# Rows of the softmax maximum on SP's queue and one slot sooner, and a pool bank for the value products of each unit

## The chip, the cores and the metric

The kernel runs on one core of one Trainium2 chip. Its time is in device microseconds. A core has TensorE (PE in the profile, with PEld for its weight loads), VectorE (DVE), ScalarE (ACT), GpSimd (POOL) and SyncE (SP). SP computes nothing here; it issues DMA transfers. ScalarE can issue transfers too, between its computations.

## The reference

Four layers one after the other on x of 2048 x 512 in float32, each with a layer norm ahead and a residual sum: a spectral mixing layer, an attention layer, and both once more with the same weights.

```
def _A_ref(x, dft_seq_re, dft_seq_im, dft_hid_re, dft_hid_im):
    a = jnp.einsum("bsd,ed->bse", x, dft_hid_re)
    b = jnp.einsum("bsd,ed->bse", x, dft_hid_im)
    y = jnp.einsum("ts,bse->bte", dft_seq_re, a) - jnp.einsum("ts,bse->bte", dft_seq_im, b)
...
for s in range(N):                                   # N = 4 segments of L = 512 rows, H = 32 heads of 16
    qs, ks, vs = q[:, :, s], k[:, :, s], v[:, :, s]
    logits = jnp.einsum("bhqd,bhkd->bhqk", qs, ks) * scale + mask
    p = _softmax(logits, axis=-1)
    a_dot = jnp.einsum("bhqk,bhkd->bhqd", p, vs)
    a_mem = (phi(qs) @ M) / (phi(qs) @ z + 1e-6)
    o = g * a_mem + (1.0 - g) * a_dot
    M, z = M + phi(ks)^T vs, z + sum(phi(ks))
```

The change touches the attention layers alone: the softmax inside a segment.

## The kernel before, in words

**Units and slots.** An attention layer has 4 segments (`NSEG`), in each 4 groups of 8 heads (`NG`, `HG`), and in each group 2 units of 4 heads (`HU`): 32 units a layer, 64 in all. The program is written as generators, and `place(order, gen, *slots)` puts each step of a generator into a numbered slot; the steps of a slot are issued by rising `order`. A unit n has the slots t to t + 9 with t = t0 + 10 n (`SU` = 10), but its steps reach far around them. TensorE executes exactly in this program order (`in_order`, L80). The instructions of the other engines and of the queues are put in order by the framework's planner, which keeps the dependences, goes by program order and by priority (`tc.high_priority`), and plays the program through with estimated durations. Each queue then works strictly in its order: a transfer at the head of SP's queue that waits holds up all behind it.

**The steps of a unit.**
- `stack` (L787), slot t - 22: four transfers on SP (L803) bring 48 rows of query parts and of key parts to each half ("side", at partitions 0 and 64) of the tiles `stkq` and `stkk`. A query tile has three buffers; three key tiles take turns. Two heads share a side.
- `natural_max` (L810), slots t - 18, - 16, - 14, - 12, - 10: TensorE makes the scores with the queries on the partitions (tile `nat`), VectorE masks each block and reduces it to its row minimum of negated scores (L834, tile `mx`, 4 heads x 4 blocks of 128 rows). In slot t - 8 two VectorE operations (L848, L849) write the maximum as a high part and a remainder into `parts` (`mparts` in the profile). The tile has 5 copies of 16 columns; only two are written, the other three hold zeros.
- `max_rows` (L855), slot t - 4 (t - 5 for the very last unit): TensorE turns the 80 columns of `parts` into rows (tile `mT`), ScalarE copies 32 of them to `mt` (L864), and four transfers on ScalarE's queue (L868), one for each side and part, lay them as row 48 or 49 under the queries of `stkq`. The keys have rows of ones there, so the next product subtracts the maximum.
- `softmax_values` (L874), slots t to t + 12: TensorE makes the scores with the keys on the partitions, with the two extra rows (tile `sT`, five rounds in slots t, t + 2, t + 4, t + 6, t + 8); ScalarE clamps the diagonal blocks (L900) and takes the exponential (L901, tile `pT`); GpSimd zeroes above the diagonal (L904). In slot t + 12 the value products (`pv`, L914) gather the 4 heads in one bank of PSUM, each head in 17 of its 32 partitions (16 values and a column of ones, for the row sum), and ScalarE copies the bank to `ot` (L966).
- `output` (L975), slot t + 14: `ot` is turned back, divided by the row sum and weighted.

**What lies between.** The slots are filled with the projections (`proj`, tiles `pqk`, whose split results go out through SP on L779), the values (`values`, `pvv`), the memory terms and the output product (`po`). Loads and stores of rows are on SP as well.

**The value bank.** PSUM has 8 banks in one pool (`bank`, L114). `alloc_pv` (L1146) takes one at the start of an attention layer and clears it on VectorE (L1148); every unit of the layer accumulates into this one bank, and the 15 partitions of each head that no product writes keep the zeros. The other 7 banks go round among all else.

**The values' tile.** `v_all` (L175) holds six row blocks of 32 x 17 numbers; `ones` (L1282) sets the columns of ones on GpSimd at the start of the first attention.

Of the kernel before, what the change touches and what calls it, by code (L numbers as in the profile page):

```python
# [10 lines left out]
F32 = mybir.dt.float32  # L11
# [23 lines left out]
NSLOT = 3  # L35
KROWS = NSLOT * DH
MROWS = 2
MCOPIES = 5
SIDES = (0, 64)
HP = 2  # L40
VW = DH + 1
# [17 lines left out]
def spectral_infini_kernel(  # L59
# [111 lines left out]
    def finish(ps, xr, x_out, i):  # L171
        V.tensor_tensor(out=xr, in0=ps, in1=xr, op=ALU.add)
        nc.sync.dma_start(x_out[i], xr)

    v_all = consts.tile([P, 6, H * VW], F32, name="v_all")  # L175
    v_tiles = [v_all[:, i].rearrange("p (h e) -> p h e", e=VW) for i in range(6)]
    spare = v_all.rearrange("p a b -> p (a b)")[:, : 6 * 512].rearrange("p (a b) -> p a b", b=512)
    v_count = [0]
    max_parts = [
        consts.tile([P, MCOPIES, HU, LT], F32R, name=f"mparts{i}") for i in range(2)  # L180
    ]

    slots = {}
# [496 lines left out]

    def place_attention(x_in, x_out, t0, w_at, out_at):
        ws, xT, vt, o_nat, state, scr, phi, stacks, maxima, outs = ({} for _ in range(10))
        k_stacks, pv_banks = [], []

        def prep(s, n):
            xt = [load_rows(x_in[s * LT + i]) for i in n]
# [24 lines left out]
        def values(s):  # L711
            vt[s] = {}
            for i in (0, 1, 3, 2):
                ps = bank("pvv")
                for d in range(DT):
                    matmul3(
                        ps,
                        lambda h: xT[s][:, h, d, i * P : (i + 1) * P],
                        lambda h: ws["v", d][:, h, :],
                        d == 0,  # L720
                        d == DT - 1,
                    )
                    if d + 1 < DT:
                        yield
                v = v_tiles[v_count[0] % len(v_tiles)]
                v_count[0] += 1
                A.activation(v[:, :, :DH], ps.rearrange("p (h d) -> p h d", d=DH), AF.Copy)
                vt[s][i] = v
                yield
# [80 lines left out]
        def natural_max(s, g, u):  # L810
            qs, ks = stacks[s, g, u, "q"], stacks[s, g, u, "k"]
            mx = sb.tile([P, HU, LT], F32, name="mx", bufs=2)

            def scores(*cols):
                banks = [bank("nat") for _ in SIDES]
                views, off = [], 0
                for p, i in cols:
                    n = (i + 1) * P
                    for a, at in enumerate(SIDES):
                        T.matmul(  # L820
                            banks[a][:, off : off + n],
                            qs[at : at + KROWS, p, i * P : (i + 1) * P],
                            ks[at : at + KROWS, p, :n],
                            start=True,
                            stop=True,
                        )
                        h = a * HP + p
                        views.append((banks[a][:, off : off + n], mx[:, h, i : i + 1]))
                    off += n
                for src, dst in views[::2] + views[1::2]:  # L830
                    n = src.shape[1]
                    junk = sb.tile([P, 512], BF16, name="junk", bufs=1)
                    with tc.high_priority(offset=URGENT):
                        last_max[0] = V.tensor_tensor_reduce(  # L834
                            junk[:, :n], src, mask[:, 512 - n :], 1.0, 3e38,
                            ALU.add, ALU.min, dst,
                        )

            for p in range(HP):
                scores((p, 3))  # L840
                yield
                scores((p, 0), (p, 2))
                yield
            scores((0, 1), (1, 1))
            yield
            parts = max_parts[((s * NG + g) * (HG // HU) + u) % 2]
            with tc.high_priority(offset=2 * URGENT):
                V.tensor_scalar(parts[:, 0], mx, -1.0, None, op0=ALU.mult)  # L848
                V.scalar_tensor_tensor(  # L849
                    parts[:, 1], mx, -1.0, parts[:, 0].bitcast(F32), op0=ALU.mult, op1=ALU.subtract  # L850
                )
            maxima[s, g, u] = parts
            yield

        def max_rows(s, g, u):  # L855
            qs, parts = stacks[s, g, u, "q"], maxima.pop((s, g, u))
            pt = bank("mT")
            T.transpose(
                pt[: MCOPIES * HU * LT, :P], parts.rearrange("p a h i -> p (a h i)").bitcast(F32), ident
            )  # L860
            n = MROWS * HU * LT
            mt = sb.tile([P, P], F32R, name="mt", bufs=2)
            with tc.high_priority(offset=URGENT):
                A.activation(mt[:n], pt[:n, :P], AF.Copy)  # L864
            for a, at in enumerate(SIDES):
                for r in range(MROWS):
                    j = (r * HU + a * HP) * LT
                    nc.scalar.dma_start(  # L868
                        qs[at + KROWS + r : at + KROWS + r + 1].rearrange("p h s -> p (h s)").bitcast(F32),
                        mt[j : j + HP * LT].bitcast(F32),  # L870
                    )
            yield

        def softmax_values(s, g, u):  # L874
# [39 lines left out]
            def pv(pv_bank, kt, pt, off):  # L914
                n = 512 - kt * P
                for h in range(HU):
                    T.matmul(
                        pv_bank[32 * h : 32 * h + VW, kt * P :],
                        vt[s][kt][:, h0 + h, :],
                        pt[h % HP][:, h // HP, off : off + n],  # L920
                        start=kt == 0,
                        stop=kt == 2,
                        skip_group_check=True,
                    )
# [32 lines left out]
            ev(0, third)  # L957

            def last():
                pb = pv_banks[0]  # L960
                pv(pb, 0, p0, 0)
                pv(pb, 1, p1, 0)
                pv(pb, 3, p1, 384)
                pv(pb, 2, [p2[0][:, :, p] for p in range(HP)], 0)
                ot = sb.tile([P, 512], F32, name="ot", tag="ut", bufs=8)
                A.activation(ot, pb, AF.Copy)  # L966
                outs[s, g, u] = ot
# [175 lines left out]
            finish(ps, xr, x_out, s * LT + i)  # L1143
            yield

        def alloc_pv():  # L1146
            pv_banks.append(bank("pv_bank"))
            V.memset(pv_banks[0], 0.0)  # L1148
            yield

        def alloc_out(s):
            o_nat[s] = [pair("onat", "wd", 8, F32) for _ in range(LT // 2)]
            yield
# [7 lines left out]
        def unit(n):  # L1161
            return n // USEG, n % USEG // NU, n % NU
# [11 lines left out]
        for k in range(4 * DT):  # L1174
            n, d = "qkvo"[k // DT], k % DT
            src = rows((wq, wk, wv, wo)[k // DT], d)
            place(3, load_split(ws, (n, d), src, f"w{n}", "w", 16), [w_at(k) - 3, w_at(k)])
        place(0.1, alloc_pv(), [t0])
        for n in range(NSEG * USEG):
            t = t0 + SU * n  # L1180
            place(0, softmax_values(*unit(n)), run_from(t, 13))
            place(1.9, output(*unit(n)), [t + 14])
            place(1.9, max_rows(*unit(n)), [t - (5 if x_out is out_tiles and n == NSEG * USEG - 1 else 4)])
            place(1, natural_max(*unit(n)), run_from(t - 18, 5, 2), [t - 8])
            place(0.5, stack(*unit(n)), [t - 22])
        for s in range(NSEG):
            b = t0 + SS * s
# [65 lines left out]
    def setup():  # L1253
        nonlocal ident, mask, same_head, gate
        with tc.issue_after(later[0].ins):
            ident = consts.tile([P, P], F32, name="ident")
            make_identity(nc, ident)
            mask = consts.tile([P, 512], BF16, name="mask")
            G.memset(mask, 0.0)
            G.affine_select(  # L1260
                mask[:, 384:], mask[:, 384:], pattern=[[-1, P]], compare_op=ALU.is_ge,
                fill=MASK, base=0, channel_multiplier=1,
            )
            same_head = consts.tile([P, HG], F32, name="same_head")
            V.tensor_reduce(
                same_head, ident.rearrange("p (d h) -> p h d", h=HG), op=ALU.add, axis=mybir.AxisListType.X
            )

            for t in max_parts:
                G.memset(t[:, MROWS:].bitcast(F32), 0.0)  # L1270
            gate = consts.tile([P, 2, H], F32, name="gate")
            beta_b = consts.tile([P, H], F32, name="beta_b")
            nc.sync.dma_start(beta_b, beta[None, :].to_broadcast([P, H]))
            eb = beta_b
            A.activation(eb, beta_b, AF.Exp, scale=-1.0)
            V.tensor_scalar_add(eb, eb, 1.0)
            V.reciprocal(gate[:, 0], eb)
            V.tensor_scalar(gate[:, 1], gate[:, 0], -1.0, 1.0, op0=ALU.mult, op1=ALU.add)
        yield

    ident = mask = same_head = gate = None
    def ones():  # L1282
        for v in v_tiles:
            G.memset(v[:, :, DH:], 1.0)
        yield

    place(5, setup(), [200])
# [46 lines left out]
```

## Time and profile before

| | us |
|---|---|
| time, median of 3 runs | 2052.89 |
| lowest and highest | 2046.74, 2054.2 |
| the profiled execution's own time | 2052.54 |
| its span, first to last instruction | 2050.8 |
| TensorE busy | 1854.5 |
| VectorE busy | 1390.6 |
| ScalarE busy | 1079.4 |
| GpSimd busy | 356.0 |

Both spectral layers and both attentions stand in this span one after another; the attentions fill about 430 to 1020 us and 1450 us to the end. In a line of the profile a name such as `sT<-stkq,stkk` gives the tile that is written and those that are read. "PE sT L84 <- DMA stkq<-mt" in a list of waits reads: TensorE, about to write `sT`, stood idle until a transfer from `mt` to `stkq` had landed; behind it stand the sum in us, the number of times, and the longest. "ACTq" and "SPq" are transfers being issued by ScalarE's and SP's sequencers; such a line lasts as long as the issue, not until the data has landed. "PEclk" and the granted clock are the share of the full clock that TensorE was given.

### The profile page before, as it was taken

The page shows a single profiled execution, that of the slowest core. Times are in us where ns is not written, and L with a number is a line of the kernel's source. Part 1 is how long each engine was busy: PE and PEld are TensorE (multiplying, and loading weights), DVE is VectorE, ACT ScalarE, POOL GpSimd, SP SyncE. Part 2 cuts the span into 40 slices and gives each one's busy share as a digit, 9 for nine tenths or more (in the row PEclk, how much of TensorE's full clock was granted, in tenths as well). Part 3 has the DMA queues.
Part 4 walks back from the last instruction along what each step waited for, and adds up shares of the span by engine and source line. Part 5 has one row for each costly group of instructions (what it writes and reads, how often), then busy time and mean ns, then how long its engine had stood idle before and what let it go on. Part 6 is the DMA issues. An engine that isn't in the chain of part 4 may idle for free.

```text
span 2050.8 us, 32671 instructions
## 1 busy us (share of the span) xinstructions
PE 1854.5 (90%) x10192; PEld 1308.2 (64%) x10192; DVE 1390.6 (68%) x4116; ACT 1079.4 (53%) x2388; POOL 356.0 (17%) x667
## 2 busy tenths in 40 slices
PE   8999999997889889887899999999878898898878
PEld 6888778874455555554578878888545555565444
DVE  8988878745567658656678986575565576676554
ACT  3344434326666556555564664443356575566544
POOL 1000000022222223324210000002122232332222
PEclk9999999998899989998899999999988999899878
DMA  8777753544433434334467776555443353253331
GB/s 278 256 256 237 247 184 122 175 144 135 109 88 114 127 79 130 104 79 115 136 197 239 256 238 194 160 154 166 124 120 98 75 151 99 82 142 101 97 68 37
DMA packets 147292, 303.12 MB, mean 148 GB/s; under 512 B 19888, under 2 KB 23984, under 8 KB 147120
## 3 DMA queue, kind: packets, MB, share of 16 engines
q1 hardware_dynamic: 136112, 287.39, 46.8%
q10 hardware_dynamic: 11008, 13.64, 1.9%
q8 instruction: 82, 1.34, 0.3%
q14 instruction: 90, 0.74, 0.1%
HBM read 211.83 MB, written 88.08 MB: 146 GB/s over the span
## 4 chain that ended last, share of the span: by engine, by line
PE 33%; DMA 5%; ACT 5%; DVE 3%; ACTq 2%; issue 2%; POOL 0%; DVEq 0%
PE m L84 13%; DMA stkq<-mt 5%; PE pv_bank L84 5%; PE y L84 4%; PE pqk L84 3%; ACT pT L901 2%; PE sT L84 2%; PE po L84 2%; ACTq L868 2%; PE pvv L84 1%; PE nat L84 1%; DVE junk L834 1%; ACT sT L900 1%; PE oT L84 0%; PE on L84 0%
## 5 line engine op out<-in xcount | busy, mean ns | idle before, releaser
L834 DVE CUSTOM_DVE_ANT_0 junk<-nat,mask 128x512 bf16<-128x512 f32 (+3 forms) x1024 | 497.2, 486 | 412.4 <-PE nat L84 362.8
L901 ACT ACTIVATE pT<-sT 128x512 f32<-128x512 f32 x640 | 350.0, 606 | 5.7 <-DMA stkq<-mt 5.0
L84 PE MATMUL sT<-stkq,stkk 50*128 50x256 f32 (+3 forms) x1024 | 191.1, 390 | 157.5 <-DMA stkq<-mt 139.3
L904 POOL TENSOR_SCALAR_AFFINE_SELECT pT<-pT 128x256 f32<-128x256 f32 (+1 forms) x448 | 193.2, 445 | 771.4 <-ACT pT L901 622.8
L84 PE MATMUL m<-chi,xa 128*128 128x512 f32 x1056 | 309.1, 393 | 2.7 <-DVE c L524 2.1
L900 ACT ACTIVATE sT<-sT 128x256 f32<-128x256 f32 x625 | 179.6, 329 | 191.4 <-PE sT L84 117.4
L84 PEld LDWEIGHTS sT<-stkq,stkk 50*128 50x128 f32 x1024 | 99.3, 195 | 283.8 <-issue 144.4
L84 PE MATMUL m<-clo,xa 128*128 128x512 f32 x720 | 230.6, 392 | 5.2 <-DVE clo L100 5.2
L84 PEld LDWEIGHTS m<-chi,xa 128*128 128x128 f32 x1056 | 198.0, 188 | 46.8 <-DVE c L524 2.9
L84 PE MATMUL pv_bank<-pT,v_all 128*17 128x512 f32 (+3 forms) x2048 | 188.4, 515 | 0.0
L84 PE MATMUL y<-wdt,us 128*128 128x512 f32 x768 | 182.5, 391 | 0.2 <-DVE wdt L100 0.2
L84 PE MATMUL nat<-stkk,stkq 48*128 48x512 f32 (+3 forms) x1024 | 168.3, 358 | 3.0 <-DVE mx L834 1.8
L84 PEld LDWEIGHTS y<-wdt,us 128*128 128x128 f32 x768 | 143.4, 188 | 30.7 <-DVE wdt L100 0.9
L84 PEld LDWEIGHTS m<-clo,xa 128*128 128x128 f32 x720 | 135.3, 188 | 37.5 <-DVE clo L100 9.8
L98 ACT ACTIVATE chi<-cring 128x512 fp32r<-128x512 f32 (+1 forms) x138 | 99.7, 727 | 85.8 <-PE m L84 35.4
L966 ACT ACTIVATE ot<-pv_bank 128x512 f32<-128x512 f32 x64 | 38.2, 598 | 195.2 <-PE pv_bank L84 195.2
L84 PEld LDWEIGHTS pv_bank<-pT,v_all 128*17 128x17 f32 x2048 | 59.6, 109 | 124.7 <-issue 121.5
L84 PE MATMUL pqk<-xT,wq 128*128 128x512 f32 x384 | 127.7, 457 | 0.0
L84 PE MATMUL pvv<-wv,xT 128*128 128x512 f32 x384 | 126.5, 454 | 0.0
L84 PEld LDWEIGHTS nat<-stkk,stkq 48*128 48x128 f32 x1024 | 110.6, 202 | 20.0 <-issue 5.7
L84 PE MATMUL po<-wo,oh 128*128 128x512 f32 x384 | 119.2, 433 | 1.5 <-ACT mt L864 0.7
L84 PE MATMUL pqk<-xT,wk 128*128 128x512 f32 x384 | 113.5, 425 | 0.8 <-ACT parts L764 0.7
(187 smaller groups left out, 2831.2 us busy)
## 6 DMA issues: line engine op xcount, KB each, us to landing
cring<-in_ct SPq DMA_DIRECT2D x97, 256.0 KB
scrk<-parts SPq DMA_DIRECT2D x96, 256.0 KB
stkq<-scrq SPq DMA_DIRECT2D x128, 192.0 KB
stkk<-scrk SPq DMA_DIRECT2D x128, 192.0 KB
cring<-sum SPq DMA_DIRECT2D x95, 256.0 KB
xt<-mid SPq DMA_DIRECT2D x64, 256.0 KB
scrq<-parts SPq DMA_DIRECT2D x32, 512.0 KB
cring<-in_ct SPq DMA_DIRECT2D x27, 512.0 KB
```

Of the source, the lines that this page charges most:

```text
L84: return tc.keep_in_program_order(op(*args, **kwargs))
L98: pin(A.activation(hi, src, AF.Copy, scale=scale))
L834: last_max[0] = V.tensor_tensor_reduce(junk[:, :n], src, mask[:, 512 - n :], 1.0, 3e38, ALU.add, ALU.min, dst,)
L868: nc.scalar.dma_start(qs[at + KROWS + r : at + KROWS + r + 1].rearrange("p h s -> p (h s)").bitcast(F32), mt[j : j + HP * LT].bitcast(F32),)
L900: A.activation(blocks, blocks, AF.Relu)
L901: A.activation(dst[a], ps, AF.Exp, scale=-SCALE)
L904: G.affine_select(blocks, blocks, pattern=[[0, n] for n in blocks.shape[1:-1]] + [[1, P]], compare_op=ALU.is_ge, fill=0.0, base=0, channel ...
L966: A.activation(ot, pb, AF.Copy)
```

## The change

Three things at once.

1. `max_rows` issues two transfers on SP in place of four on ScalarE's queue. To let one transfer carry both parts of a side, `parts` is laid out by side, part, head and block, so that 16 turned rows in a row belong to one side; the VectorE operations write it with a stride. The tile has 72 columns instead of 80, of which 32 are used as before.
2. `max_rows` stands in slot t - 5 instead of t - 4 (t - 6 instead of t - 5 for the very last unit), and the last step of `natural_max`, the two VectorE operations, in t - 9 instead of t - 8.
3. The value products of each unit take a bank from the pool, and none is held through the layer. So that every partition of it is written, the products use 32 columns of the values, the head's 17 and 15 of the next head's, which nobody reads; `v_all` gets 15 columns of zeros at its end for the last head. The clearing of the bank goes.

```
-MCOPIES = 5
+MCOLS = 72
...
-    v_all = consts.tile([P, 6, H * VW], F32, name="v_all")
+    v_all = consts.tile([P, 6, H * VW + 32 - VW], F32, name="v_all")
...
-        consts.tile([P, MCOPIES, HU, LT], F32R, name=f"mparts{i}") for i in range(2)
+        consts.tile([P, MCOLS], F32R, name=f"mparts{i}") for i in range(2)
...
-                v = v_tiles[v_count[0] % len(v_tiles)]
+                j = v_count[0] % len(v_tiles)
+                v, v_flat[s, i] = v_tiles[j], v_all[:, j]
...
+            sides = mx.rearrange("p (a b) i -> p a (b i)", b=HP)
+            both = parts[:, : MROWS * HU * LT].rearrange("p (a r j) -> p a r j", a=2, r=MROWS)
+            hi, lo = (both[:, :, r] for r in range(MROWS))
...
-                V.tensor_scalar(parts[:, 0], mx, -1.0, None, op0=ALU.mult)
+                V.tensor_scalar(hi, sides, -1.0, None, op0=ALU.mult)
                 V.scalar_tensor_tensor(
-                    parts[:, 1], mx, -1.0, parts[:, 0].bitcast(F32), op0=ALU.mult, op1=ALU.subtract
+                    lo, sides, -1.0, hi.bitcast(F32), op0=ALU.mult, op1=ALU.subtract
                 )
...
-                pt[: MCOPIES * HU * LT, :P], parts.rearrange("p a h i -> p (a h i)").bitcast(F32), ident
+                pt[:MCOLS, :P], parts.bitcast(F32), ident
...
             for a, at in enumerate(SIDES):
-                for r in range(MROWS):
-                    j = (r * HU + a * HP) * LT
-                    nc.scalar.dma_start(
-                        qs[at + KROWS + r : at + KROWS + r + 1].rearrange("p h s -> p (h s)").bitcast(F32),
-                        mt[j : j + HP * LT].bitcast(F32),
-                    )
+                n = MROWS * HP * LT
+                nc.sync.dma_start(
+                    qs[at + KROWS : at + KROWS + MROWS].rearrange("p h s -> p (h s)").bitcast(F32),
+                    mt[a * n : (a + 1) * n].bitcast(F32),
+                )
...
-                        pv_bank[32 * h : 32 * h + VW, kt * P :],
-                        vt[s][kt][:, h0 + h, :],
+                        pv_bank[32 * h : 32 * (h + 1), kt * P :],
+                        v_flat[s, kt][:, (h0 + h) * VW : (h0 + h) * VW + 32],
...
-                pb = pv_banks[0]
+                pb = bank("pv_bank")
...
-        def alloc_pv():
-            pv_banks.append(bank("pv_bank"))
-            V.memset(pv_banks[0], 0.0)
-            yield
...
-        place(0.1, alloc_pv(), [t0])
...
-            place(1.9, max_rows(*unit(n)), [t - (5 if x_out is out_tiles and n == NSEG * USEG - 1 else 4)])
-            place(1, natural_max(*unit(n)), run_from(t - 18, 5, 2), [t - 8])
+            place(1.9, max_rows(*unit(n)), [t - (6 if x_out is out_tiles and n == NSEG * USEG - 1 else 5)])
+            place(1, natural_max(*unit(n)), run_from(t - 18, 5, 2), [t - 9])
...
-        for v in v_tiles:
+        for j, v in enumerate(v_tiles):
             G.memset(v[:, :, DH:], 1.0)
+            G.memset(v_all[:, j, H * VW :], 0.0)
```

More of the change, by code (lines that the diff above doesn't have):

```diff
@@ L173, in finish @@
         nc.sync.dma_start(x_out[i], xr)
-    v_all = consts.tile([P, 6, H * VW], F32, name="v_all")
-    v_tiles = [v_all[:, i].rearrange("p (h e) -> p h e", e=VW) for i in range(6)]
+    v_all = consts.tile([P, 6, H * VW + 32 - VW], F32, name="v_all")
+    v_tiles = [v_all[:, i, : H * VW].rearrange("p (h e) -> p h e", e=VW) for i in range(6)]
     spare = v_all.rearrange("p a b -> p (a b)")[:, : 6 * 512].rearrange("p (a b) -> p a b", b=512)
@@ L682, in place_attention @@
         ws, xT, vt, o_nat, state, scr, phi, stacks, maxima, outs = ({} for _ in range(10))
-        k_stacks, pv_banks = [], []
+        k_stacks, v_flat = [], {}
         def prep(s, n):
@@ L1269, in setup @@
             for t in max_parts:
-                G.memset(t[:, MROWS:].bitcast(F32), 0.0)
+                G.memset(t[:, MROWS * HU * LT :].bitcast(F32), 0.0)
             gate = consts.tile([P, 2, H], F32, name="gate")
```

## The prediction

> **What bounds the kernel now.** I read the page's span first, then the busy time by stage, the waits of TensorE, the tile of the copied maxima, the timeline of one unit and the chain of waits through it.
>
> ```profile
> span 2050.8 us, 32671 instructions
> ```
>
> ```profile
> 430.00:1020.00 590.00, 502.95 (x3194) 311.76 (x3193) 373.68 (x1475) 344.11 (x849) 161.33 (x302) 0.90 0.40 110
> 1020.00:1450.00 430.00, 428.13 (x1945) 346.64 (x1945) 311.72 (x598) 218.34 (x415) 22.78 (x29) 1.00 0.62 198
> 1450.00:2050.80 600.80, 508.75 (x3256) 312.25 (x3255) 361.44 (x1434) 345.99 (x850) 152.29 (x300) 0.89 0.36 99
> ```
>
> The columns are the stage, its length, the busy time of PE, PEld, DVE, ACT and POOL, the granted clock, the DMA share and GB/s. Between the attentions (second row) TensorE is idle for 1.9 us of 430, at clock 1.00. In the two attentions it is idle for 87 and 92 us, at clocks 0.90 and 0.89, and no other engine is busy for more than 64% of them. The change touches attention alone, so the question is what ends these 179 us:
>
> ```profile
> PE sT L84 <- DMA stkq<-mt: 139.3, 70, 4.4
> ...
> PE sT L84 <- ACT phi L756: 4.8, 2, 2.4
> ```
>
> One wait holds 139.3 us: the first softmax scores of a unit wait for the rows of the maximum, 70 times, 2.0 us each. The next in attention has 4.8. Who moves these rows, and how slowly:
>
> ```profile
> L868 ACTq DMA_DIRECT2D stkq<-mt x256: 627/627/1237, 453.1 to 2020.9; - x128
> ```
>
> ```profile
> 1874.97 0.94 PE L84 MATMUL pvv<-wv,xT 128*128 128x512 f32 x3
> ...
> 1877.01 0.31 PE L84 MATMUL mT<-ident,mparts 128*80 128x128 f32 x1
> ...
> 1877.35 0.27 ACT L864 ACTIVATE mt<-mT 32x128 fp32r<-32x128 f32 x1 [0.47 <-PE mT L84]
> ...
> 1878.32 1.97 ACTq L868 DMA_DIRECT2D stkq<-mt  x3
> ...
> 1879.15 0.32 SPq L803 DMA_DIRECT2D stkk<-scrk  x1
> 1879.57 0.88 SPq L803 DMA_DIRECT2D stkq<-scrq  x2
> 1880.50 0.62 SPq L803 DMA_DIRECT2D stkk<-scrk  x1
> ...
> 1884.32 0.47 PE L84 MATMUL sT<-stkq,stkk 50*128 50x256 f32 x3 [1.62 <-DMA stkq<-mt]
> ...
> 1889.16 0.45 PE L84 MATMUL nat<-stkk,stkq 48*128 48x512 f32 x2
> ```
>
> ```profile
> 1879.65 4.53 DMA stkq<-mt
> ...
> 2007.69 2.29 DMA stkq<-mt
> ...
> 2020.93 1.76 DMA stkq<-mt
> ```
>
> The copy ends at 1877.62. The fourth transfer is issued at 1879.65, 2.0 us later, and lands 4.53 after that, at 1884.18. Its landing runs beside the four stack loads that SP issues from 1879.15 to 1881.12. In the last two units, after which no stack is loaded, the same step takes 2.29 and 1.76. So three things make the rows late: four issues in a row, the stack loads beside them, and the late turn.
>
> **The change part by part.**
>
> *One slot sooner.* In TensorE's order the turn moves ahead of slot 5's products and slot 6's scores, by 1877.01 - 1874.97 = 2.04 us. The maxima must be split by then:
>
> ```profile
> 1868.91 0.17 DVE L849 SCALAR_TENSOR_TENSOR mparts<-mx,mparts 128x16 fp32r<-128x16 f32 x1
> ```
>
> They are ready at 1869.08, 5.9 us ahead of the new turn, so the turn waits for nothing new. The two VectorE operations also stand one slot sooner; their count and size stay, so they cost nothing more. On ScalarE the copy (0.27 us) goes ahead of some exponentials; it is the same work in another order.
>
> *Two transfers instead of four, on SP.* ScalarE issues 256 transfers at 0.627 us each, 160 us of its queue in all, and drops them. This gives TensorE nothing by itself, as ScalarE is not the bound. SP takes 128. No row has a transfer of this shape on SP; the nearest are ACT's own 0.627 and this larger one:
>
> ```profile
> L418 ACTq DMA_DIRECT2D sum<-cring x11: 326/327/373, 230.6 to 324.8; - x11
> ```
>
> I take 0.63 (0.33 to 1.25, were it to grow with the doubled rows). In the unit above: turn at 1874.97, copy done by about 1875.8 (ScalarE may finish an exponential first), second issue started by 1876.5, landed 2.3 later, 1878.8, as the stack loads are issued only from 1879.15. TensorE asks for the rows at 1884.32 - 1.62 = 1882.70. Cover: 3.9 us; with a slow landing of 4.53 still 1.7.
>
> The Trainium skill, "DMA: Bandwidth & Descriptors", section "Why a DMA increments its semaphore by 16 and not by 1", speaks against this shape: a transfer is spread over the largest number of engines up to 16 that divides the slowest dimension of both sides. By it one row from eight went over 8 engines, and two rows from sixteen go over 2, eight pieces each in turn. No view here shows the spread of one transfer. If eight pieces in turn doubled the 2.29 us landing, an estimate, the sum would still hold in this unit; only units with less than 2.3 us of cover would pay, at most 64 x 0.5 us or so, and the sum by the page would be some 30 us higher.
>
> *What SP's queue holds.* SP takes its transfers in order, so the rows can stand behind a store that waits, and the stack loads behind the rows.
>
> ```profile
> 1894.17 2.06 SPq L779 DMA_DIRECT2D scrq<-parts  x2
> ...
> 1894.90 0.25 ACT L864 ACTIVATE mt<-mT 32x128 fp32r<-32x128 f32 x1
> ```
>
> ```profile
>   POOL pT L904: 7.0, 2
> ```
>
> In units with a query projection two such stores sit at SP's head until 1894.17 and end at 1896.23. Rows behind them would start there: later than the copy, yet ahead of or level with the fourth issue of today. The stack loads come up to 2 x 0.63 = 1.3 us later; nothing on TensorE waits for them now (who waited for line 803: only the row shown). I set both at nothing. If that cover goes, it is the first rival's price.
>
> *What goes of the wait.* By this cover all 139.3 us can go. I let a quarter come back as other waits (units at either end of an attention, banks, ScalarE's order), a choice: -139.3 x 0.75 = -104.
>
> *The granted clock.* Two units of nearly the same work:
>
> ```profile
> 1850.60:1869.50 18.90, 15.55 (x102) 9.66 (x105) 10.85 (x47) 11.37 (x28) 6.92 (x12) 0.91 0.44 142
> 1886.50:1903.10 16.60, 13.94 (x98) 8.53 (x97) 10.09 (x44) 11.39 (x28) 6.31 (x12) 1.00 0.45 140
> ```
>
> The first is idle for 3.35 us, the second for 2.66. Busy time goes about as one over the clock: 15.55 x 0.91 = 14.2. Were attention at 1.00 as the stage between is, TensorE would save 502.95 x 0.10 + 508.75 x 0.11 = 106 us. With the stalls gone I expect three quarters of it: -80. The Trainium skill, "TensorE: Matmul & The Clock Gate", Part 1, says that the clock halves after an idle window of about 3.4 us. By that, stalls of 2.0 us would hardly lower it, it would not come back with them, and the sum would be 80 us higher. The trace agrees in part: 2.66 idle us left the clock at 1.00 above, yet the stage means are 0.90 and 0.89 with a longest stall of 4.4.
>
> *The value products.* 32 columns of weights instead of 17:
>
> ```profile
> L84 PEld LDWEIGHTS pv_bank<-pT,v_all x2048: 92/98/155, 474.6 to 2039.0; 128*17 128x17 f32 x187
> ```
>
> ```profile
> L84 PEld LDWEIGHTS mT<-ident,mparts x64: 115/118/120, 452.4 to 2017.9; 128*80 128x80 f32 x64
> ```
>
> 80 columns take 118 ns, 17 take 98, so 32 take at most 20 more: 2048 x 0.020 = 41 us if each showed, a quarter of it with four heads side by side, and by the columns' share 15 of 63 about 2.5. The bank is no longer held: the pool has eight for everyone else, but the first value product of a unit may wait for one.
>
> ```profile
> PEld sT L84 <- DVE mx L834: 19.4, 36, 1.9
> ```
>
> Such a weight load waits 0.5 us on the mean now. Bounds: -19 (those waits go) to +64 x 0.5 = +32. I take +5 for both together. The two clears of the bank, the six clears of padding on GpSimd and 72 instead of 80 turned columns: one answer, nothing.
>
> *Sum.* -104 - 80 + 5 = -179. The profiled execution took 2052.54 us (span 2050.8 and 1.7 around it), 0.4 from the median of 2052.89. 2052.5 - 179 = 1873.5, say **1873 us**.
>
> **The rivals.**
>
> *Slower: the rows end up behind the stack loads in SP's order.* Should the planner put them there, they start after 1881.12 and the second at about 1881.8; with 4.53 to land, 1886.3 against 1884.18. That is +2.1 us x 64 = +134, 2187 us, and it decides once the first issue falls behind 1879.15 in most units. For it: that order is the planner's, nobody wrote it. Against it: the copy would be done 3.3 us before these loads are released.
>
> *The next wait takes half.* ScalarE and VectorE are busy for 11.39 and 10.09 us of 16.60 in the fast unit; at 14 us a unit, ScalarE has 81%. And the stack loads have 10.0 us from issue (1879.15) to first use (1889.16), which shrinks by the stall and the clock to 8 or less, with 4.5 or more to land. If half of the wait returns and a third of the clock's share comes: -70 - 35 + 5 = -100, 1952 us.
>
> *The clock stays at 0.90*, because something other than these stalls sets it: -104 + 5, 1953 us. For it: the unit with 2.66 idle us ran at 1.00. Against: the stage between runs at 1.00 with a busier TensorE.
>
> *Nothing moves*: the rows come sooner and another engine's lateness, now hidden behind them, is as long. About 2050. Against it: no wait but this one has over 4.8 us.
>
> **How the numbers follow.** The forecast has 0.64, the two rivals near 1950 together 0.23, no change 0.05, slower 0.08. Of the forecast's own bounds the lower is the whole wait and the whole clock, 2052.5 - 139 - 106 = 1808; the upper, with half of the clock's share and the bank's 32, is about 1930. The range reaches on over the two rivals near 1950, with the value products' remaining bound (41 - 5 = 36): 1808 to 1990. Faster by over 0.5% (about what a measurement of this kernel can tell from no change) is 0.64 + 0.23 = 0.87, within it 0.05, slower 0.08.
>
> **What would show it.** Right: no softmax score waits for the rows, or for under 20 us in all; landing under 3 us from issue; the clock in both attentions above 0.96; both attention stages together near 1191 - 179 = 1012 us. Wrong: issues of the rows behind the stack loads on SP; value products or natural scores that wait for banks or stack loads by over 0.5 us a unit; a clock of 0.90 without the stalls.

## The result, and the profile after

| | before | after |
|---|---|---|
| time, median of 4 runs each, us | 2051.74 | 1786.52 |
| lowest and highest | 2046.74, 2054.2 | 1784.13, 1787.75 |
| the profiled execution | 2052.54 | 1787.75 |
| mean granted clock over the span | 0.940 | 0.993 |

The ratio is 0.8709, 95% interval 0.8689 to 0.8728: 265 us fewer. The forecast of 1873 us had the sign and the mechanism, but 86 us too little of it; 1786.5 lies 21.5 us below the low end of the range, 1808.

First the page's span and busy time, then the stages. The edges are chosen so that each row holds the same number of matmuls, to within four, as its row of before (3194, 1945 and 3256 there).

```profile
span 1786.0 us, 32579 instructions
...
PE 1745.4 (98%) x10192; PEld 1266.5 (71%) x10192; DVE 1383.1 (77%) x4114; ACT 1071.3 (60%) x2388; POOL 357.7 (20%) x673
```

```profile
430.00:890.00 460.00, 450.41 (x3195) 291.48 (x3193) 369.47 (x1473) 339.72 (x847) 163.35 (x303) 0.99 0.53 141
890.00:1320.00 430.00, 428.16 (x1945) 346.73 (x1944) 312.49 (x596) 219.44 (x418) 22.64 (x29) 1.00 0.63 199
1320.00:1786.00 466.00, 452.15 (x3260) 290.78 (x3258) 357.95 (x1437) 342.06 (x850) 152.73 (x300) 0.99 0.48 127
```

The stage between the attentions is the same 430 us. The attentions went from 590.0 + 600.8 to 460 + 466, that is 1190.8 to 926: the whole gain, 264.8, where 1012 was forecast. Inside them TensorE's idle time fell from 87.1 + 92.1 to 9.6 + 13.9, by 155.7, and its busy time from 502.95 + 508.75 to 450.41 + 452.15, by 109.1, at clocks of 0.99 after 0.90 and 0.89. Now the waits of TensorE:

```profile
PE xnT L84 <- DVE xn L168: 6.1, 5, 1.7
PE nat L84 <- DMA stkk<-scrk: 5.6, 8, 2.2
...
PE pv_bank L84 <- DVE mx L835: 1.7, 1, 1.7
...
PE sT L84 <- DMA stkq<-mt: 0.8, 2, 0.5
```

The 139.3 us of waiting for the rows are 0.8, and no wait of that size took their place. The stack loads, for which TensorE never waited before, are now late 8 times, 5.6 us in all. The issues, and a values unit like the one in the prediction:

```profile
L871 SPq DMA_DIRECT2D stkq<-mt x128: 598/617/785, 452.6 to 1758.0; - x128
```

```profile
1652.55 0.27 PE L84 MATMUL mT<-ident,mparts 128*72 128x128 f32 x1
...
1653.31 0.26 ACT L868 ACTIVATE mt<-mT 32x128 fp32r<-32x128 f32 x1
...
1653.60 1.29 SPq L871 DMA_DIRECT2D stkq<-mt  x2
...
1656.66 0.32 SPq L804 DMA_DIRECT2D stkk<-scrk  x1
...
1657.08 0.84 SPq L804 DMA_DIRECT2D stkq<-scrq  x2
...
1657.97 0.41 SPq L804 DMA_DIRECT2D stkk<-scrk  x1
...
1659.84 0.50 PE L84 MATMUL sT<-stkq,stkk 50*128 50x256 f32 x4
```

The copy ends at 1653.57, SP issues both transfers by 1654.89, the first stack load only follows at 1656.66, and the first score runs at 1659.84: 6.3 us after the copy. So it is everywhere: in each of the 64 units SP issues the first of the two within 0.03 us of the end of the copy, and nothing stands ahead of them in its queue. The chain of waits has the landing itself in the last unit alone, beside no stack load:

```profile
1757.36 0.62 SPq L871
...
1758.03 1.92 DMA stkq<-mt
...
1760.09 0.47 PE sT L84 x3
```

### The profile page after: what moved, and what is told of

It is laid out like the page before. It is cut to its first block, busy times and chain, and to the rows that moved or that the text cites. A ratio compares the mean times of both kernels' runs of the same rounds, so it can differ in the third digit from the quotient of the medians.

```text
span 1786.0 us, 32579 instructions
## 1 busy us (share of the span) xinstructions
PE 1745.4 (98%) x10192; PEld 1266.5 (71%) x10192; DVE 1383.1 (77%) x4114; ACT 1071.3 (60%) x2388; POOL 357.7 (20%) x673
## 3 DMA queue, kind: packets, MB, share of 16 engines
q1 hardware_dynamic: 138416, 288.44, 54.7%
q10 hardware_dynamic: 6912, 12.59, 1.8%
## 5 line engine op out<-in xcount | busy, mean ns | idle before, releaser
L84 PE MATMUL nat<-stkk,stkq 48*128 48x512 f32 (+3 forms) x1024 | 159.2, 345 | 8.4 <-DMA stkk<-scrk 5.6
L84 PE MATMUL sT<-stkq,stkk 50*128 50x256 f32 (+3 forms) x1024 | 164.8, 373 | 1.0 <-DMA stkq<-mt 0.8
L84 PEld LDWEIGHTS sT<-stkq,stkk 50*128 50x128 f32 x1024 | 84.4, 186 | 113.4 <-issue 53.0
L84 PE MATMUL pv_bank<-pT,v_all 128*32 128x512 f32 (+3 forms) x2048 | 152.2, 437 | 1.7 <-DVE mx L835 1.7
L84 PEld LDWEIGHTS pv_bank<-pT,v_all 128*32 128x32 f32 x2048 | 59.2, 110 | 84.1 <-issue 82.8
L84 PE MATMUL pqk<-xT,wq 128*128 128x512 f32 x384 | 116.9, 425 | 0.0
L84 PEld LDWEIGHTS nat<-stkk,stkq 48*128 48x128 f32 x1024 | 96.5, 189 | 27.2 <-ACT pT L904 7.7
L147 POOL TENSOR_TENSOR r<-ve,half_neg 128x2 f32<-128x2 f32 (+2 forms) x24 | 19.9, 830 | 472.9 <-DVE ve L145 469.5
L84 PE MATMUL pvv<-wv,xT 128*128 128x512 f32 x384 | 114.1, 417 | 0.0
L84 PE MATMUL pqk<-xT,wk 128*128 128x512 f32 x384 | 108.5, 410 | 2.0 <-DVE mx L835 2.0
```

The costliest lines, as they stand in the source:

```text
L84: return tc.keep_in_program_order(op(*args, **kwargs))
L147: G.tensor_tensor(out=r, in0=ve, in1=half_neg[:, :n], op=ALU.pow)
```

## The experiments

The theory: lateness of the rows at the head of a unit is what TensorE stood idle for, and the clock falls with those stalls. Its rivals: ScalarE, held up by the issues, is the next to be late; the number of transfers or the queue matters by itself; the clock has another cause; the bank is worth something. All ratios are to the kernel before on the same chip, with 95% intervals. Idle is the span less TensorE's busy time in the profiled execution; before has 1854.5 and 196.3, after 1745.4 and 40.6. Lines of the code shift by a few between kernels: the exponentials are line 900, 901, 903 to 906, the moved rows 868, 871 or 873.

| kernel | us | ratio | clock | busy, idle of TensorE |
|---|---|---|---|---|
| e1: two on SP alone | 1815.82 | 0.8827 (0.8794 to 0.8861) | 0.988 | 1762.5, 51.3 |
| e2: the slot alone | 1922.32 | 0.934 (0.9293 to 0.9387) | 0.967 | 1821.6, 103.1 |
| e3: the bank alone | 2065.15 | 1.0036 (1.0011 to 1.0061) | 0.933 | 1857.4, 205.9 |
| e4: all but the bank | 1798.83 | 0.8748 (0.8715 to 0.8781) | 0.993 | 1757.2, 39.9 |
| e5: after, four on SP | 1811.28 | 0.8818 (0.8785 to 0.8851) | 0.989 | 1758.8, 50.6 |
| e6: after, two on ScalarE | 1808.61 | 0.88 (0.8767 to 0.8833) | 0.991 | 1761.8, 45.3 |
| e10: after, a late turn | 2174.71 | 1.0589 (1.0544 to 1.0634) | 0.911 | 1872.2, 302.7 |
| e11: after, held bank, 32 columns | 1801.31 | 0.8775 (0.8752 to 0.8797) | 0.993 | 1755.2, 41.5 |
| e12: after, four on ScalarE | 1873.29 | 0.9123 (0.9096 to 0.9149) | 0.982 | 1788.1, 83.2 |
| e13: after again | 1784.07 | 0.8692 (0.8668 to 0.8715) | 0.995 | 1742.3, 40.0 |
| e14: e4 again | 1799.7 | 0.8761 (0.8737 to 0.8786) | 0.995 | 1754.5, 41.1 |
| e15: after, one norm turn later | 1785.77 | 0.8705 (0.8683 to 0.8727) | 0.994 | 1744.5, 39.3 |

**e1, two transfers on SP alone** (old slot, held bank, 17 columns), against before:

```
-                for r in range(MROWS):
-                    j = (r * HU + a * HP) * LT
-                    nc.scalar.dma_start(
+                n = MROWS * HP * LT
+                nc.sync.dma_start(
...
```

> Two transfers on SP alone: turn in the old slot, value bank held, 17 columns. Theory (the rows' landing time is all that counts): copy done near 1877.6 in the unit of the prediction, second issue over by 1878.9, ahead of the stack loads, landed near 1880.9 against a demand at 1882.7, so units with values lose their wait; in units with a query projection the rows stand behind two stores on SP and are 0 to 1 us late. TensorE's wait for the rows 0 to 30 us, clock over 0.96, 1790 to 1850 us. Rival 1 (SP's queue holds the rows up): a wait of 60 us or more, 1900 us or more. Rival 2 (the slot is what counts): 1950 us or more.

```profile
PE sT L84 <- DMA stkq<-mt: 6.9, 12, 1.7
```

The wait falls to 6.9 us with the turn where it was, and the time is where the theory had it. 241 of the 265 us are here, though the parts will turn out not to add.

**e2, the slot alone** (four on ScalarE, held bank), against before:

```
-            place(1.9, max_rows(*unit(n)), [t - (5 if x_out is out_tiles and n == NSEG * USEG - 1 else 4)])
-            place(1, natural_max(*unit(n)), run_from(t - 18, 5, 2), [t - 8])
+            place(1.9, max_rows(*unit(n)), [t - (6 if x_out is out_tiles and n == NSEG * USEG - 1 else 5)])
+            place(1, natural_max(*unit(n)), run_from(t - 18, 5, 2), [t - 9])
```

> One slot sooner alone: four transfers on ScalarE's queue, value bank held. Theory: rows land 2.0 us sooner plus some tenths for less of the stack loads beside them, demand at 1882.7 against a landing near 1881.5 to 1882.1: the wait falls to 20 to 60 us, the clock rises to about 0.96, 1800 to 1900 us. Rival 1 (four issues in ScalarE's queue hold up the exponentials, which then end the wait): 1950 us or more with ScalarE named in TensorE's waits. Rival 2 (the slot alone does it): under 1795 us.

The waits of TensorE, then those who waited behind the issues of the rows, from their tile, and the longest such line of before:

```profile
PE nat L84 <- ACT parts L764: 17.6, 20, 1.5
PE nat L84 <- ACT pT L901: 13.7, 15, 1.4
PE nat L84 <- DVE mx L834: 10.2, 22, 0.9
...
PE sT L84 <- DMA stkq<-mt: 6.7, 6, 1.8
```

```profile
  ACT pkn L1048: 49.2, 18
  ACT praw L763: 46.2, 17
  ACT sT L900: 17.3, 7
  ACT pT L901: 11.6, 5
```

```profile
  ACT sT L900: 67.5, 33
```

The rows are in time here as well (6.7 us), but the time is 107 us above e1. ScalarE itself stood still behind its own four issues for over 120 us. It did so in before too, for 104, but there it was mostly the clamps of the scores that stood behind them, and here it is copies out of PSUM (`praw` from `pqk`, `pkn` from `pkT`). Natural scores, which need the banks that ScalarE empties, became late: TensorE waits for ScalarE for 52.9 us in all, against 12.7 in before and 3.6 in e1. The rival named ScalarE's issues rightly, though with the exponentials behind them, which have 11.6 us, and with 1950 us or more; the theory's 1800 to 1900 was missed.

**e3, the bank and the 32 columns alone** (after's layout of the parts, four on ScalarE, old slot), against before:

```
-                        pv_bank[32 * h : 32 * h + VW, kt * P :],
-                        vt[s][kt][:, h0 + h, :],
+                        pv_bank[32 * h : 32 * (h + 1), kt * P :],
+                        v_flat[s, kt][:, (h0 + h) * VW : (h0 + h) * VW + 32],
...
-                pb = pv_banks[0]
+                pb = bank("pv_bank")
```

> The bank from the pool and 32 columns alone: four transfers on ScalarE's queue in the old slot (the columns of the maxima keep the new layout, 72 of them). Theory (the bank has no part while the rows are late): 2040 to 2060 us, wait for the rows about 139 us. Rival (the held bank made the pool short): under 2000 us.

```profile
PE sT L84 <- DMA stkq<-mt: 152.3, 82, 4.3
```

By itself it brings nothing: 1.0036, if anything 7 us slower. The wait for the rows is 13 us longer; the cause stays open, and the layout of the parts, which differs too, is not parted from the bank here.

**e4, all but the bank**, against after (e14 the same once more):

```
-                        pv_bank[32 * h : 32 * (h + 1), kt * P :],
-                        v_flat[s, kt][:, (h0 + h) * VW : (h0 + h) * VW + 32],
+                        pv_bank[32 * h : 32 * h + VW, kt * P :],
+                        vt[s][kt][:, h0 + h, :],
...
-                pb = bank("pv_bank")
+                pb = pv_banks[0]
```

> All of the change but the bank: two transfers on SP, one slot sooner, value bank held and 17 columns. Theory: 1785 to 1800 us, no wait for the rows. Rival (with the wait gone the pool of seven is what is late next): 1820 us or more, with weight loads or products waiting for VectorE or ScalarE to empty banks.

e1 and e4 ran on the same chip, and differ by the slot alone: 17 us. Against after, 0.8748 and 0.8709 have intervals that overlap, so the bank was measured again below.

**e5, four on SP, and e6, two on ScalarE**, against after:

```
-                nc.sync.dma_start(
-                    qs[at + KROWS : at + KROWS + MROWS].rearrange("p h s -> p (h s)").bitcast(F32),
-                    mt[a * n : (a + 1) * n].bitcast(F32),
-                )
+                for r in range(MROWS):
+                    j = a * n + r * HP * LT
+                    nc.sync.dma_start(
+                        qs[at + KROWS + r : at + KROWS + r + 1].rearrange("p h s -> p (h s)").bitcast(F32),
+                        mt[j : j + HP * LT].bitcast(F32),
+                    )
```

```
-                nc.sync.dma_start(
+                nc.scalar.dma_start(
```

> The changed kernel with four transfers on SP instead of two, one for each side and part as before the change. Theory (what counts is that ScalarE's queue is rid of them; SP has room): 1783 to 1800 us, no wait for the rows, the stack loads 1.3 us later at most. Rival (the number of transfers counts): 1820 us or more, with the rows or the stack loads late by the two further issues.

> The changed kernel with its two transfers on ScalarE's queue instead of SP's. Theory (with the rows early enough, ScalarE's issue time is the next bound; 128 issues of 0.63 us, 80 us in all, are half of what the sooner turn alone was left with): between the changed kernel and the sooner turn alone, 1815 to 1870 us, with natural scores and weight loads that wait for ScalarE to empty banks, and a clock near 0.98. Rival (two transfers are as good on any queue): under 1800 us.

The issues of e5, from its tile, and its wait for the rows; then the issues of e6:

```profile
L873 SPq DMA_DIRECT2D stkq<-mt x256: 634/635/767, 453.4 to 1780.0; - x128
```

```profile
PE sT L84 <- DMA stkq<-mt: 5.7, 7, 1.1
```

```profile
L871 ACTq DMA_DIRECT2D stkq<-mt x128: 620/621/1241, 453.6 to 1777.9; - x128
```

An issue costs 0.62 to 0.64 us on either queue, one row or two. By the ratios the number (four for two, on SP) costs 0.011 of 2052, some 22 us, and the queue (ScalarE for SP, two each) 0.009, some 19. Both sides missed on e5, theory with 1783 to 1800 and rival with 1820 or more; e6 fell between them. The intervals of both stand clear of after's. In e5 TensorE is idle for 10 us more than in after, 4.9 of it for the rows and 5.2 for ScalarE (7.7 against 2.5), and busy for 13.4 us more. The mean clock, 0.989 against 0.993, would make some 7 of these, an estimate; the rest stays open.

**e10, a late turn**, against after:

```
-            place(1.9, max_rows(*unit(n)), [t - (6 if x_out is out_tiles and n == NSEG * USEG - 1 else 5)])
+            place(1.9, max_rows(*unit(n)), [t - 2])
```

> The changed kernel with the turn in slot t - 2 instead of t - 5, all else as changed: it makes TensorE wait for the rows again, with nothing on ScalarE's queue. Theory (the low clock is the stalls' own doing): two slots are 2.7 us, copy, two issues and landing take 4.3 to 5, so 1.6 to 2.5 us of wait a unit, 100 to 160 us; the clock of the attentions falls back to 0.90 to 0.95 and TensorE's busy time rises by 50 to 110 us; 1930 to 2060 us. Rival (the low clock came from something else that the change took away, such as ScalarE's issues): the wait comes back but the clock stays over 0.98 and the busy time under 1765 us; 1880 to 1950 us.

The waits, the copy and SP's queue in one unit with the chain through it, and the two attentions:

```profile
PE sT L84 <- DMA stkq<-mt: 273.1, 67, 6.7
```

```profile
774.49 0.31 SPq L804 DMA_DIRECT2D stkk<-scrk  x1
...
774.96 0.78 SPq L804 DMA_DIRECT2D stkq<-scrq  x2
...
775.46 0.25 ACT L868 ACTIVATE mt<-mT 32x128 fp32r<-32x128 f32 x1
...
775.78 0.43 SPq L804 DMA_DIRECT2D stkk<-scrk  x1
...
776.31 1.28 SPq L871 DMA_DIRECT2D stkq<-mt  x2
```

```profile
776.31 4.98 DMA stkq<-mt
...
781.43 0.96 PE sT L84 x4
```

```profile
430.00:1075.00 645.00, 508.53 (x3172) 318.58 (x3171) 365.04 (x1463) 337.51 (x836) 159.82 (x298) 0.85 0.37 100
1520.00:2170.00 650.00, 507.04 (x3216) 314.38 (x3215) 348.87 (x1407) 342.94 (x848) 152.17 (x300) 0.85 0.33 87
```

Two things are shown at once. The clock falls to 0.85 with the stalls, with no row on ScalarE's queue. And the rows now stand behind the four stack loads: issue to score is over 5 us, against 2.7 in after's last unit. That is the order of the prediction's slower rival, but not its case: here the copy itself ends late, at 775.71, with three of the four loads issued, and the order adds the 0.6 us to 776.31; the rival had the sooner turn. So its price of 2187 us lies near the 2174.7 by luck. The expectation had 1930 to 2060: it took 4.3 to 5 us for copy, issues and landing and 2.7 us from the turn to the demand. This unit has 5.8 (775.46 to 781.29) and 1.7 (the turn starts at 774.68, and TensorE stands from 776.38).

**e11, the held bank with 32 columns, beside e13, after again, e14, and e12, four on ScalarE**, all on one chip. e12's edit is that of e5 with `nc.scalar`; e11's, against after:

```
-                pb = bank("pv_bank")
+                pb = pv_banks[0]
...
+            pv_banks.append(bank("pv_bank"))
+            V.memset(pv_banks[0], 0.0)
```

> The changed kernel with the value bank held through the layer, but with the 32 columns: it parts the bank from the columns. Theory (the bank counts, the 15 further columns cost nothing): as slow as with the held bank and 17 columns, within 3 us. Rival (the columns cost something): 5 us or more slower than that.

> The changed kernel with four transfers on ScalarE's queue: the fourth corner beside two on SP (1786), four on SP (1811) and two on ScalarE (1809). Theory (ScalarE held up for 2.5 us a unit is late for the banks it has to empty, which two issues barely cause): far above the sum of the two, 1880 to 1925 us, with TensorE's waits for ScalarE at 30 us or more and the granted clock near 0.97. Rival (number and queue simply add): 1825 to 1845 us.

> The changed kernel once more, as the measure for the other kernels beside it on the same chip: 1783 to 1790 us.

> All of the change but the bank, once more, beside the changed kernel: theory (with the wait gone, the eighth bank is worth something) 8 to 15 us slower than the changed kernel; rival (the difference seen was the spread between chips) within 4 us of it.

e11 and e14 differ by the 15 columns alone and agree within 2 us: the columns cost nothing that can be measured. Both are slower than e13, by 17.2 and 15.6 us, and the intervals stand apart: the bank taken per unit is worth about 16. Weight loads of the softmax scores that wait for exponentials, in e14 and then in e13:

```profile
PEld sT L84 <- ACT pT L904: 26.9, 74, 0.5
```

```profile
PEld sT L84 <- ACT pT L904: 13.0, 37, 0.4
```

With one bank more to go round, half as many of these loads wait for ScalarE, 13.9 us less. But the same loads' idle time with no wait in view ("issue") is 13.0 us more, 52.7 in e13 against 39.7 in e14, so these lines do not show how the bank brings its 16 us; that stays open. e12:

```profile
PE sT L84 <- DMA stkq<-mt: 24.1, 17, 2.1
...
PE nat L84 <- DVE mx L835: 6.8, 15, 0.9
PE nat L84 <- ACT parts L765: 5.4, 8, 0.8
```

Four issues on ScalarE cost 89 us beside e13, and by the ratios some 63 more than the same four on SP (e5). Number and queue by themselves cost 22 and 19, 41 together, and the rival that added them up (1825 to 1845) was wrong; the theory, with 1880 to 1925, missed by 7. Its mechanism is half of the story: of the 43 us that TensorE idles more than in e13, 23 are for the rows, which are late again, and 17 for ScalarE (18.4 in all, where the theory had 30 or more). In e12's tile pkn and pT stand behind the issues for 22.0 and 20.7 us, where after and e5 have no ScalarE operation behind them at all. e2 has the same slot and four issues with the held bank and the old layout, and its ratio is 0.022 higher, some 45 us; that it is the bank that softens it is argued, as the layout differs too.

**e15, one turn of the layer norm later**, against after, for the longest wait that attention has left:

```
-                place(2, prep(s, (2 * j, 2 * j + 1)), [*(t - d for d in first), t, t, t + 2])
+                place(2, prep(s, (2 * j, 2 * j + 1)), [*(t - d for d in first), t, t, t + (3 if s == 1 else 2)])
```

> The changed kernel with the second turn of each pair of normalised rows in segment 1 one slot later (t + 3 instead of t + 2), so that VectorE has another slot for them: the largest waits left in the attentions (TensorE for xn, 6 to 7 us in 5 waits of up to 1.7, followed by halved clocks at 505 and 1379 us). Theory (a stall costs itself and up to half of the halved clock behind it): 4 to 10 us faster than the changed kernel, 1774 to 1780 us, ratio to the kernel before near 0.865. Rival (the turned rows are then late for the projections, or VectorE is simply behind): the same or slower, 1784 us or more.

```profile
PE xnT L84 <- DVE xn L168: 5.9, 3, 2.4
```

The wait was 6.1 and is 5.9, and the ratio 0.8705 is after's within the noise, as the rival had it.

## Why the prediction was wrong, and where it was right

*What bounds the kernel: right.* The wait for the rows was the bound in attention. Either change that makes them sooner removes it by itself (6.9 us left in e1, 6.7 in e2), which is why the parts do not add: 241 and 135 us less, and 7 more, against 265 together. That e2 gains so much less than e1 is taken up below.

*The three causes of the lateness, and the order on SP: right.* The rows are issued ahead of the stack loads, land in 1.92 us in the last unit, and have 3 us of cover in the unit shown (1654.89 and some 2 for landing, an estimate from that 1.92, against 1659.84; the prediction worked out 3.9). Behind the stack loads, as in e10, the landing took 4.98.

*The clock: right in kind.* It returns as the stalls go, and rival three (it stays at 0.90) falls with after and e10 together. The table above has it in one row after another: 40 us idle at 0.993 to 0.995, 51 at 0.988, 83 at 0.982, 103 at 0.967, 196 at 0.940 in before, 206 at 0.933, 303 at 0.911.

*The step that failed: the two three-quarters, beside a relief of ScalarE counted as nothing.* "I let a quarter come back as other waits (units at either end of an attention, banks, ScalarE's order), a choice" had no row behind it, and the same quarter was withheld from the clock. The traces settle each term:

| term, us | forecast | measured |
|---|---|---|
| the wait for the rows | -104 | 0.8 - 139.3 = -138.5 |
| other idle time of the attentions | 0 | -155.7 + 138.5 = -17.2 |
| the clock | -80 | 502.95 x 0.09 + 508.75 x 0.10 = -96 |
| value products and bank | +5 | -109.1 + 96 = -13 |
| sum | -179 | -264.8 |

The clock's share goes by the forecast's own rule with the measured 0.99; what is left of the busy time, 13, is near the 12.2 us by which e14 is busier than e13. These two are good to some 5 us only: with the trace's clocks to three digits (0.905 and 0.891 before, 0.989 and 0.988 after) the clock has 92 and the rest 17. The 86 us that the forecast fell short are some 34.5 of the wait, 17 of other waits, 16 of the clock and 18 of the bank. Nothing came back: the other waits shrank, where the withheld quarter had them grow.

The quarter is not made of nothing, though: e2 shows it. There the wait for the rows falls by 132.6 us (139.3 to 6.7), and 196.3 - 132.6 = 63.7 us of idle time should be left; 103.1 are. So 39 us, three tenths, came back, and TensorE's waits for ScalarE rose by 40. In e1, with two issues on SP in place of the four on ScalarE, the same working leaves 63.9 and the trace has 51.3. The prediction withheld the quarter for "ScalarE's order" among others, and in the same text counted the 160 us of issues that ScalarE drops as nothing; by e1 and e2, that relief is what kept the quarter from coming back. The waits of before could not tell the two cases apart, because a lateness that is hidden behind the rows stands in no line of them.

*The range.* Its floor, 1808, was the whole wait and the whole clock, but left out the gain of 19 that the text itself gave as the bank's bound: 2052.5 - 139 - 106 - 19 = 1788. That this meets the profiled 1787.75 is luck: the 17 us of other waits, for which no term stood, make up for a clock and a bank that fell short of their bounds by 10 and 6. A floor has to take in every bound of the sum, the small terms with them.

*"This gives TensorE nothing by itself, as ScalarE is not the bound": wrong.* It could hold only while the late rows hid ScalarE's lateness. With the rows in time (1.0 us of waiting) two issues on ScalarE cost 19 us (e6). Four cost 89 beside e13 (e12), the rows being late again in part. In before ScalarE was busy for 58% of the attentions (344.11 of 590.00 us and 345.99 of 600.80); such a share does not show that its queue issues for 2.5 us in a row (four times 0.63), with the copies that empty banks behind it.

*The columns, the stores ahead of the rows, the spread over fewer engines: right to cost nothing.* The value products take 437 ns each and their weight loads 110; in e14, with 17 columns, 434 and 97. As to the stores, the prediction had the rows wait behind them in units with a query projection; that case never came, as the rows go out within 0.03 us of the copy.

## What to carry to other kernels

Where one wait holds most of the idle time (139 of 179 us here) and the next has a thirtieth of it, ask whether the change also relieves the engine that would be late next. Where it does (e1, after), the whole wait went, and what the clock owes to it; where it does not (e2), three tenths came back. Small transfers issued from an engine that also computes hold up what stands behind them there, even where its busy share is below 60%; here they were cheaper on a queue that does nothing else, and in fewer issues. Two changes that cure the same wait did not add, and a part that is worth nothing while another wait hides it (the bank) can be worth 16 us when that wait is gone.

## What the runs showed of the hardware

*The clock falls after windows that are far from idle.* Four stretches of after, with a wait of 2.21 us for a stack load that ends at 1718.51:

```profile
1713.70:1717.10 3.40, 2.60 (x37) 1.19 (x29) 3.15 (x14) 2.48 (x7) 0.63 (x1) 1.00 0.92 184
1717.10:1720.50 3.40, 1.99 (x10) 1.53 (x12) 1.05 (x6) 0.69 (x2) 0.76 (x2) 1.00 0.17 28
1720.50:1723.90 3.40, 3.40 (x16) 2.35 (x14) 2.51 (x14) 1.90 (x5) 0.76 (x2) 0.50 0.15 55
1723.90:1727.30 3.40, 2.85 (x20) 1.71 (x21) 2.86 (x11) 2.77 (x8) 1.28 (x3) 1.00 0.46 108
```

TensorE is busy for 1.99 of the second stretch's 3.40 us, and the clock is 0.50 for the whole of the next, though that one is busy throughout. The Trainium skill, "TensorE: Matmul & The Clock Gate", Part 1, has free-running windows of 3.4 us and a halved clock after an idle one. The trace agrees in the length of the windows, 3.4 us, and not in the condition: 1.4 idle us of 3.4 were enough here. They are not always enough. On the same grid, counted in windows of 3.41 us from the end of a halved stretch of before at 1869.21, the stall of 1.62 us in the prediction's unit puts 1.45 idle us into one window, and the next is at 1.00:

```profile
1882.87:1886.28 3.41, 1.96 (x13) 1.58 (x13) 1.18 (x6) 1.69 (x5) 0.00 (x0) 1.00 0.41 70
1886.28:1889.69 3.41, 3.41 (x41) 1.45 (x40) 1.00 (x7) 0.84 (x3) 0.64 (x1) 1.00 0.00 0
```

Counted over both attentions of before in this way, all 32 windows with 2.0 idle us or more were followed by a halved one, and of the 27 with 1.4 to 2.0 it was 17. What decides between these is open. So a stall of 2 us in every unit can cost more than itself, by up to 1.7 us for each halved window, an estimate; by the table above the clock had 96 us over 64 units, 1.5 us each.

*Two rows in one transfer landed about as soon as one row.* Packets on SP's and ScalarE's queues, of before and then of after:

```profile
q1 hardware_dynamic: 136112, 287.39, 46.8%
q10 hardware_dynamic: 11008, 13.64, 1.9%
```

```profile
q1 hardware_dynamic: 138416, 288.44, 54.7%
q10 hardware_dynamic: 6912, 12.59, 1.8%
```

256 transfers took 11008 - 6912 = 4096 packets, 16 each; 128 take 138416 - 136112 = 2304, 18 each. Either queue has the same counts (e5 on SP 16, e6 on ScalarE 18). By the rule of the Trainium skill that the prediction weighed ("DMA: Bandwidth & Descriptors", "Why a DMA increments its semaphore by 16 and not by 1"), that is eight pieces and eight completions, and sixteen pieces and two completions; the counts agree with it, and the engines themselves stand in no view. The price that the rule might have had does not show in the few landings beside no stack load: two rows, by the rule over two engines, in 1.92 us, one row, over eight, in 1.76 and 2.29.
